# Scores in four quarters of the array, and a ring for the transposed probabilities, in a fused attention and feed-forward kernel

## The chip, the core and the metric

The kernel runs on one core of one Trainium2 chip. A core has five engines that run beside each other and wait for each other through semaphores: TensorE (PE: matrix multiplications into PSUM, with its weight loads PEld), VectorE (DVE), ScalarE (ACT), GpSimd (POOL) and SyncE (SP), which issues DMAs. The metric is the device time of one execution in microseconds (us); lower is better.

## What is computed

```python
scores = scale * np.matmul(q, k.transpose(0, 1, 3, 2))      # batch 8, heads 8, seq 576, head_dim 64
kth = np.partition(scores, -32, axis=-1)[..., -32:-31]
scores = np.where(scores >= kth, scores, -1e9)
attn = np.exp(scores - scores.max(-1, keepdims=True))
attn = attn / (attn.sum(-1, keepdims=True) + 1e-9)
x = np.matmul(attn, v)          # then (B,H,S,D) -> (B*S, H*D): 4608 x 512
h = x @ w_in                    # 512 x 2048
return (h * np.cos(h)) @ w_out  # 2048 x 512
```

Each row of scores keeps its 32 largest of 576; all else gets probability zero. All data is float32, and q, k and v reach the kernel with their axes already arranged (head_dim first for q and k).

## The kernel before

**Units and blocks.** The 4608 tokens are cut into 36 blocks of 128. A block has four units, one for each pair of heads; the 144 units go one after another. A sequence has 576 tokens, which is four and a half blocks, so 4 of the 36 blocks span two batches; their units have two entries in `parts` (64 rows of one batch, 64 of the next), all others have one.

**Scores.** `scores` (L229) computes a unit's 128 x 576 scores for two heads. The first 448 keys go to the PSUM tile `sc` (two buffers of two banks), the last 128 keys to the tile `rim` (two banks, shared). Per head one matmul contracts 64 rows of the array: for a usual unit the tile is 64*128 (64 rows of the array, all 128 columns), and the two heads use the upper and the lower rows. A unit of a two-batch block does it per batch: four matmuls of 64*64. In the traces each float32 matmul shows as two instructions. `take_scores` (L244) copies them to SBUF on ScalarE: L246 for `sc`, L250 for `rim`, where a two-batch unit has two copies of 64 rows and a usual one a single copy of 128 rows.

**Search and probabilities.** VectorE folds the row in two halves (L258, larger of each pair; GpSimd gets the smaller ones with L274 and L283) and finds the 32 largest by rounds of MAX8 (L350) and MATCH_REPLACE8 (L355). From the bounds (L363, L370: `nd`) ScalarE masks (L377, L379) and exponentiates (L387). `split` on GpSimd (L410, L412) parts the words into 16-bit halves, with the reciprocal of the sums (`rden`, L400) added as a last column block; a DMA writes them to DRAM (L438) and a transposing DMA reads them back (L444) into `pT`, which holds ten blocks of 128 columns: nine of probabilities, the tenth (index `2 * NT + 1`) the reciprocals. The first units are turned on TensorE instead (`turn`, L426 to L434). `pT` has five buffers.

**P@V.** `values` (L453) multiplies the four units of a block with v into the free part of `rim` (L469; first `v_tail`, tile 64*64, then `v`, tile 128*64). `take_values` (L475) then makes `xT` on VectorE: for each of the four units one multiply of 128 x 128 of `rim` with the tenth block of its `pT` (L481).

**Feed-forward.** `ff1` (L514) multiplies `xT` with w_in in groups of 16 matmuls into one of two PSUM banks `mm` (L530); ScalarE reads each bank twice (L544, L546); GpSimd and ScalarE make h*cos(h) (L566, L575, L585, L592); `ff2` (L595) multiplies with w_out (L605), and ScalarE takes the result out (L615).

**Order.** Each engine works through its instructions in the order in which the program issues them, one `slot` per unit. Slot i searches unit i on VectorE, makes the probabilities of unit i-1, sends off unit i-2, and spreads the feed-forward matmuls by the fixed `plan`. Scores are made in the even slots for the two units to come. In every slot with i % 4 == 2 the scores are followed by P@V of the block whose units are i-6 to i-3 (the first block's comes in slot 5), and `take_values` stands on VectorE ahead of the last search of that slot (`topk_round`, with `ahead`). ScalarE's copies for unit i+1 come after the exponentials. The framework adds the waits: instructions on different engines that touch the same PSUM bank of a tile are kept in the order of the program, even when both only read it. In SBUF it goes by the parts of a tile that are touched.

Of the kernel before, what the change touches and what calls it, by code (L numbers as in the profile page):

```python
# [10 lines left out]
F32 = mybir.dt.float32  # L11
# [4 lines left out]
ALU = mybir.AluOpType  # L16

P = 128
# [12 lines left out]
def kernel(  # L31
# [9 lines left out]
    nc = tc.nc  # L41
    ctx.enter_context(tc.manual_schedule())
    B, H, D, S = qT.shape
    DM, DF = moe_w_in.shape
    NT = S // P
    TAIL = S - NT * P
# [8 lines left out]
    consts = ctx.enter_context(tc.tile_pool(name="consts", bufs=1))  # L55
    loads = ctx.enter_context(tc.tile_pool(name="loads", bufs=6))
    work = ctx.enter_context(tc.tile_pool(name="work", bufs=2))
# [102 lines left out]

    units = []
    for t0 in range(0, B * S, P):
        parts = []
        for i, a in enumerate((t0, t0 + TAIL)):
            b, q0 = a // S, a % S
            if parts and parts[-1][0] == b:
                parts[-1][2] = P
            else:
                parts.append([b, q0, TAIL, i * TAIL])
        for hp in range(NP):  # L170
            units.append({"hp": hp, "tok": t0, "parts": parts})
    NU = len(units)
    pairs = {}
    v_tails = []
# [3 lines left out]
    def place(hp, j):  # L178

        return (hp + j) % 2  # L180
# [39 lines left out]
    SB = 448  # L220
    rim = ps.tile([P, 2, 512], F32, tag="rim", name="rim", bufs=1)
# [3 lines left out]
    def rim_bank(r0, j):  # L225

        return j if r0 == 0 else 1 - j

    def scores(u):  # L229
        sc = u["sc"] = ps.tile([P, 2, 512], F32, tag="sc", name="sc", bufs=2)  # L230
        for to, k0, k1 in ((sc, 0, SB), (sc_ends[u["n"] % 2], SB, S)):
            for b, q0, rows, r0 in u["parts"]:
                for j in range(2):
                    d = slice(j * D, (j + 1) * D)
                    st = pairs[b, u["hp"]]
                    nc.tensor.matmul(  # L236
                        to[r0 : r0 + rows, rim_bank(r0, j) if k0 else place(u["hp"], j), 0 : k1 - k0],
                        st["q"][d, q0 : q0 + rows],
                        st["k"][d, k0:k1],
                        start=True,  # L240
                        stop=True,
                    )

    def take_scores(u):  # L244
        s = u["s"] = work.tile([P, 2, S], F32, tag="s", name="s", bufs=4)
        nc.scalar.copy(out=s[:, :, 0:SB], in_=u["sc"][:, :, 0:SB])  # L246
        ends = sc_ends[u["n"] % 2]
        for r, r0 in [(slice(0, P), 0)] if len(u["parts"]) == 1 else [(slice(0, TAIL), 0), (slice(TAIL, P), TAIL)]:
            back = rim_bank(r0, place(u["hp"], 0))
            nc.scalar.copy(out=s[r, :, SB:S], in_=ends[r, :: 1 - 2 * back])  # L250

    def fold_high(u):
# [62 lines left out]
    def topk_round(u, rnd, between=(), ahead=None):  # L315
        top, rest, lasts = u["top"], u["rest"], TOPK // 8 - 1
        end = TOPK - 1 - 8 * rnd
        at = top[:, :, end : end - 8 if rnd < lasts else None : -1, 0]
        search(
            at, rest[:, :, HS:S] if rnd == 0 else rest[:, :, 0:HS], rest[:, :, 0:HS], rnd < lasts,  # L320
            between if rnd < lasts else (),
        )
        if rnd < lasts:
            return
        del u["rest"]
        low = u.pop("low")
        for k in range(TOPK // 16):
            more = k < TOPK // 16 - 1
            if ahead and not more:
                take_values(ahead)  # L330
            search(top[:, :, 1 + 8 * k : 9 + 8 * k, 1], low, low, more, () if more else between)
# [73 lines left out]
    def split(u):  # L405
# [9 lines left out]
        )  # L415
        u["halves"] = halves

    def turn(u):

        s = u.pop("s").rearrange("p j k -> p (j k)")  # L420
        pT = u["pT"] = work.tile([P, 2 * NT + 2, P], F32, tag="pT", name="pT", bufs=5)
        for half in range(2):
            tt = ps.tile([P, 512], F32, tag="mm", name="tt", bufs=2)
            for c in range(NT):
                at = (half * NT + c) * P
                nc.tensor.transpose(tt[:, c * P : (c + 1) * P], s[:, at : at + P], ident)  # L426
            nc.scalar.copy(out=pT[:, half * NT : (half + 1) * NT], in_=tt.rearrange("p (c q) -> p c q", c=NT))
        at = 2 * NT * P
        nc.tensor.transpose(room[0][:, P : 2 * P], s[:, at : at + P], ident)
        rden = u.pop("rden")  # L430
        for j in range(2):
            lhsT = rden[:, j : j + 1].to_broadcast([P, D])
            nc.tensor.matmul(room[1][j * D : (j + 1) * D, P : 2 * P], lhsT, ident, start=True, stop=True)
        nc.scalar.copy(out=pT[:, 2 * NT :], in_=rim[:, :, 3 * P :])  # L434
# [4 lines left out]

    def transposes(u):  # L440
        rows = u.pop("rows").rearrange("q h k -> (q h) k")
        pT = u["pT"] = work.tile([P, 2 * NT + 2, P], F32, tag="pT", name="pT", bufs=5)
        words = pT.rearrange("p c q -> p (c q)").bitcast(U16)
        nc.sync.dma_start_transpose(  # L444
            out=words.rearrange("p (c q) -> p c q", c=2 * NT + 2), in_=rows
        )

    def place_of(u):

        bank, at = u["hp"] % 2, u["hp"] // 2 * P  # L450
        return bank, room[bank][:, at : at + P]
# [23 lines left out]
    def take_values(us):  # L475
        blk, hp, n = block_of[us[0]["tok"]], us[0]["hp"], len(us)
        if "xT" not in blk:
            blk["xT"] = work.tile([P, NP, P], F32, tag="xT", name="xT", bufs=2)
        for i, u in enumerate(us):
            to, o, pT = blk["xT"][:, hp + i], place_of(u)[1], u.pop("pT")  # L480
            nc.vector.tensor_tensor(out=to, in0=o, in1=pT[:, 2 * NT + 1], op=ALU.mult)  # L481
        blk["left"] -= n
        blk["tick"] = ff["tick"]

# [3 lines left out]
    t0 = 0  # L488
    for w in widths:
        blk = {"t0": t0, "w": w, "left": 0, "g": [], "gated": []}  # L490
# [205 lines left out]
    for n in range(NP, len(order)):  # L696
        i = last[order[n - 6]] if n >= 6 else 0
        load_at(max(i, 2 * NP + 2), load_qk, *order[n])
        i = last_values[order[n - 2 * NP]] if n >= 2 * NP else 0
# [11 lines left out]
    def send(x):  # L711

        split(x)
        write_halves(x)
        transposes(x)
# [8 lines left out]
    def slot(i, u, w, x, z):  # L724
# [23 lines left out]
        for m in made:  # L748
            scores(m)
# [13 lines left out]
        if i + 1 < NU:  # L763
            take_scores(units[i + 1])
# [26 lines left out]
    def drain(w, x, z):  # L791

        take_banks()
        if x:
            send(x)
        if w:
            merge_first(w)
            merge_second(w)
            bounds(w)
            distances(w)  # L800
            mask(w)
            exponentials(w)
            sums(w)
            reciprocal(w)
        forward(2)
        if z:
            values(z)
            take_values(z)
        forward(2)
# [5 lines left out]
    load_qk(0, 1)  # L815
    load_weights(3, nc.sync)
    scores(units[0])
    take_scores(units[0])
    decode_first(3)
    for i in range(NU):  # L820
        ff["now"] += 1
        wq["ready"] = wq["done"]
        u, w, x = (units[i - n] if n <= i else None for n in range(3))
# [46 lines left out]
```

## Time and profile before

| | |
|---|---|
| median of 3 runs | 1422.28 us (1421.6 to 1422.38) |
| the profiled execution's own time | 1422.95 us |
| span of its profile | 1421.2 us |
| mean granted TensorE clock | 0.985 |
| busy: TensorE, VectorE, GpSimd, ScalarE | 1365.5, 1351.6, 1166.0, 1086.1 us |
| score matmuls 64*128 / 64*64 into `sc` (instructions, busy us) | 512, 133.9 / 128, 15.5 |
| the same into `rim` | 512, 53.7 / 128, 6.4 |
| L250 copies of 128 rows / of 64 rows (number, mean ns) | 128, 376 / 32, 368 |
| L481 multiplies (number, mean ns) | 144, 283 |

A row of a time line gives start, length, engine, line, operation, output<-inputs, shape and number of merged instructions; a bracket at its end says how long the engine was idle before and what ended that. Instructions of one engine overlap a little: the next one starts before the one before has ended, so the cost of an instruction in a full stream is the distance from its start to the next start, which is less than its own length. The ends of matmuls are modelled; their starts are not. A slice is a fortieth of the span, and its digit the busy share in tenths.

### The profile page before, as it was taken

The page shows a single profiled execution, that of the slowest core. Times are in us where ns is not written, and L with a number is a line of the kernel's source. Part 1 is how long each engine was busy: PE and PEld are TensorE (multiplying, and loading weights), DVE is VectorE, ACT ScalarE, POOL GpSimd, SP SyncE. Part 2 cuts the span into 40 slices and gives each one's busy share as a digit, 9 for nine tenths or more (in the row PEclk, how much of TensorE's full clock was granted, in tenths as well). Part 3 has the DMA queues.
Part 4 walks back from the last instruction along what each step waited for, and adds up shares of the span by engine and source line. Part 5 has one row for each costly group of instructions (what it writes and reads, how often), then busy time and mean ns, then how long its engine had stood idle before and what let it go on. Part 6 is the DMA issues. An engine that isn't in the chain of part 4 may idle for free.

```text
span 1421.2 us, 30370 instructions
## 1 busy us (share of the span) xinstructions
PE 1365.5 (96%) x10304; PEld 993.8 (70%) x10304; DVE 1351.6 (95%) x5233; ACT 1086.1 (76%) x1922; POOL 1166.0 (82%) x804
## 2 busy tenths in 40 slices
PE   6558999999999999999999999999999999999998
PEld 3346677777777777777777777777777777777775
DVE  7999999999999999999999999999999999999931
ACT  7877787778877788778777887777877778877741
POOL 4778888888888888888888888888888898888810
PEclk9788999999999999999999999999999999999999
DMA  9576766656665666556665566756766565565530
GB/s 287 189 214 174 200 199 171 172 165 195 167 175 146 171 183 170 169 158 198 173 181 146 149 183 179 181 155 180 190 164 167 153 173 158 153 155 145 151 101 16
DMA packets 427437, 240.02 MB, mean 169 GB/s; under 512 B 375952, under 2 KB 392592, under 8 KB 427280
## 3 DMA queue, kind: packets, MB, share of 16 engines
q1 hardware_dynamic: 420720, 224.22, 58.9%
q10 hardware_dynamic: 6560, 13.85, 2.7%
q8 instruction: 81, 1.33, 0.4%
q14 instruction: 76, 0.62, 0.1%
HBM read 45.09 MB, written 101.19 MB: 103 GB/s over the span
## 4 chain that ended last, share of the span: by engine, by line
PE 92%; DVE 6%; ACT 1%; POOL 0%; DMA 0%; issue 0%; POOLq 0%
PE o L605 36%; PE mm L530 35%; PE rim L469 11%; PE sc L236 8%; DVE top L350 3%; PE rim L236 2%; DVE rest L355 1%; DVE rest L258 0%; DVE low L355 0%; DVE w_in L144 0%; DMA pT<-rows 0%; DVE w_out L144 0%; ACT s L387 0%; PE warm L813 0%; ACT s L379 0%; POOL w_out L154 0%
## 5 line engine op out<-in xcount | busy, mean ns | idle before, releaser
L530 PEld LDWEIGHTS mm<-xT,w_in 128*128 128x128 f32 x4608 | 538.4, 192 | 77.7 <-issue 63.7
L530 PE MATMUL mm<-xT,w_in 128*128 128x128 f32 x4608 | 540.2, 276 | 9.4 <-ACT x L546 7.8
L605 PE MATMUL o<-w_out,g 128*128 128x512 f32 x1152 | 524.7, 599 | 0.0
L350 DVE MAX8 top<-rest 128x8 f32<-128x288 f32 x1152 | 478.6, 450 | 0.0
L355 DVE MATCH_REPLACE8 rest<-top,rest 128x288 f32<-128x288 f32 x864 | 376.4, 443 | 0.0
L605 PEld LDWEIGHTS o<-w_out,g 128*128 128x128 f32 x1152 | 207.7, 190 | 218.0 <-issue 214.2
L410 POOL COPY halves<-s 128x2304 uint16<-128x2304 uint16 x140 | 294.8, 2105 | 58.6 <-ACT s L387 57.7
L350 DVE MAX8 top<-low 128x8 f32<-128x288 f32 x576 | 241.5, 448 | 0.5 <-POOL low L283 0.5
L387 ACT ACTIVATE s<-s,nd 128x576 f32<-128x576 f32 x288 | 220.2, 767 | 0.8
L283 POOL TENSOR_TENSOR low<-low,rest 128x576 int32<-128x576 int32 x141 | 199.4, 1414 | 11.1
L379 ACT ACTIVATE s<-s,top 128x576 f32<-128x576 f32 x288 | 205.4, 760 | 0.0
L274 POOL TENSOR_TENSOR low<-s 128x576 int32<-128x576 int32 x141 | 198.8, 1410 | 6.3 <-ACT s L250 6.3
L377 ACT ACTIVATE nd<-nd 128x2 f32<-128x2 f32 x144 | 29.3, 203 | 226.6 <-DVE nd L370 226.6
L575 POOL TENSOR_TENSOR x<-g,x 128x1024 f32<-128x1024 f32 x68 | 161.0, 2367 | 5.7
L592 POOL TENSOR_TENSOR g<-g,x 128x1024 f32<-128x1024 f32 x68 | 160.8, 2365 | 0.0
L236 PE MATMUL sc<-k,q 64*128 64x448 f32 (+1 forms) x640 | 149.4, 583 | 9.0 <-DVE low L266 4.5
L469 PE MATMUL rim<-pT,v 128*64 128x128 f32 (+1 forms) x2560 | 138.3, 267 | 0.0
L469 PEld LDWEIGHTS rim<-pT,v 128*64 128x64 f32 x2560 | 129.2, 139 | 6.5 <-issue 6.0
L246 ACT COPY s<-sc 128x896 f32<-128x896 f32 x144 | 128.3, 891 | 3.4 <-PE sc L236 3.4
L355 DVE MATCH_REPLACE8 low<-top,low 128x288 f32<-128x288 f32 x288 | 125.3, 443 | 0.0
L566 POOL TENSOR_SCALAR x<-x 128x1024 f32<-128x1024 int32 x68 | 71.3, 1048 | 61.4 <-ACT x L546 61.4
L258 DVE TENSOR_TENSOR rest<-sc,s 128x576 f32<-128x576 f32 x144 | 107.7, 748 | 7.0 <-ACT s L250 6.8
(54 smaller groups left out, 1243.3 us busy)
## 6 DMA issues: line engine op xcount, KB each, us to landing
rows<-halves SPq DMA_DIRECT2D x140, 640.0 KB, 3.0
out_dram<-ob ACTq DMA_DIRECT2D x36, 256.0 KB, 2.3
q<-in_q_dram SPq DMA_DIRECT2D x31, 288.0 KB, 3.4
st<-in_moe_w_in_dram SPq DMA_DIRECT2D x16, 512.0 KB, 6.9
v<-in_v_dram SPq DMA_DIRECT2D x32, 256.0 KB, 3.3
k<-in_k_dram SPq DMA_DIRECT2D x31, 144.0 KB, 3.4
k<-in_k_dram SPq DMA_DIRECT2D x32, 128.0 KB, 3.5
st<-in_moe_w_out_dram SPq DMA_DIRECT2D x8, 512.0 KB, 4.4
```

The lines of the kernel that those rows point to most:

```text
L236: nc.tensor.matmul(to[r0 : r0 + rows, rim_bank(r0, j) if k0 else place(u["hp"], j), 0 : k1 - k0], st["q"][d, q0 : q0 + rows], st["k"][d, k ...
L274: nc.gpsimd.tensor_tensor(out=u["low"].bitcast(I32), in0=s[:, :, 0:HS], in1=s[:, :, HS:S], op=ALU.add)
L283: nc.gpsimd.tensor_tensor(out=low, in0=low, in1=u["rest"][:, :, HS:S].bitcast(I32), op=ALU.subtract)
L350: nc.vector.max(to[:, j], src[:, j])
L355: nc.vector.match_replace(rest[:, j], to[:, j], src[:, j], NEG)
L379: nc.scalar.activation(out=s[:, j], in_=s[:, j], func=AF.Prelu, bias=less[:, j, 1:2], scale=1.0, alpha=FAR)
L387: nc.scalar.activation(out=s[:, j], in_=s[:, j], func=AF.Exp, bias=nd[:, j : j + 1], scale=SCALE, accum_out=den[:, j, 0:1],)
L410: nc.gpsimd.tensor_copy(out=halves[:, :, 0 : 2 * S], in_=s.rearrange("p (k h) -> p h k", h=2))
L469: nc.tensor.matmul(to[d, r], lhsT, rhs, start=(bank, j) not in begun, stop=c == NT - 1 and u in us[-2:] and r0 + rows == P,)
L530: nc.tensor.matmul(mm[:, at : at + w], w_in[f // FC][:, c, (f % FC) * P : (f % FC + 1) * P], blk["xT"][:, c], start=c == 0, stop=c == NC - 1,)
L575: nc.gpsimd.tensor_tensor(out=x, in0=g, in1=x, op=ALU.subtract)
L605: nc.tensor.matmul(o, g[:, at : at + P], w_out[f], start=f == 0, stop=f == NF - 1)
```

## The change

Every unit's scores run as four matmuls of 64*64 (each head, each 64 tokens), as those of two-batch units did; the list `halves_of` gives both halves their batch. L250's copy is made in two halves of 64 rows for every unit. The five buffers of `pT` become one tile `ring` with five parts, part n % 5 for unit n. Where units of a block lie next to each other in the ring, `take_values` multiplies four (when all four do) or two with one instruction; a pair that crosses the ring's end still takes two instructions.

```diff
+            halves_of.append((b, q0, i * TAIL))
...
-            for b, q0, rows, r0 in u["parts"]:
+            for b, q0, r0 in u["halves_of"]:
                 for j in range(2):
...
-                        to[r0 : r0 + rows, rim_bank(r0, j) if k0 else place(u["hp"], j), 0 : k1 - k0],
-                        st["q"][d, q0 : q0 + rows],
+                        to[r0 : r0 + TAIL, rim_bank(r0, j) if k0 else place(u["hp"], j), 0 : k1 - k0],
+                        st["q"][d, q0 : q0 + TAIL],
                         st["k"][d, k0:k1],
...
-        for r, r0 in [(slice(0, P), 0)] if len(u["parts"]) == 1 else [(slice(0, TAIL), 0), (slice(TAIL, P), TAIL)]:
-            back = rim_bank(r0, place(u["hp"], 0))
+        for r0 in (0, TAIL):
+            r, back = slice(r0, r0 + TAIL), rim_bank(r0, place(u["hp"], 0))
             nc.scalar.copy(out=s[r, :, SB:S], in_=ends[r, :: 1 - 2 * back])
...
+    RING = 5
+    ring = consts.tile([P, RING, 2 * NT + 2, P], F32, tag="ring", name="ring")
...
-        pT = u["pT"] = work.tile([P, 2 * NT + 2, P], F32, tag="pT", name="pT", bufs=5)
+        pT = u["pT"] = ring[:, u["n"] % RING]
...
-        for i, u in enumerate(us):
-            to, o, pT = blk["xT"][:, hp + i], place_of(u)[1], u.pop("pT")
-            nc.vector.tensor_tensor(out=to, in0=o, in1=pT[:, 2 * NT + 1], op=ALU.mult)
+        i = 0
+        while i < n:
+            at, h = us[i]["n"] % RING, (hp + i) // 2
+            m = 4 if n - i == 4 and at + 4 <= RING else 2 if at + 2 <= RING else 1
+            if m > 1:
+                o = rim[:, :, 2 * (S - SB) + h * P : 2 * (S - SB) + (h + m // 2) * P]
+                nc.vector.tensor_tensor(
+                    out=blk["xT"][:, hp + i : hp + i + m].rearrange("p (h b) q -> p h b q", b=2),
+                    in0=o.rearrange("p b (h q) -> p h b q", q=P),
+                    in1=ring[:, at : at + m, 2 * NT + 1].rearrange("p (h b) q -> p h b q", b=2),
+                    op=ALU.mult,
+                )
+            else:
+                for k in range(i, i + 2):
+                    nc.vector.tensor_tensor(
+                        out=blk["xT"][:, hp + k], in0=place_of(us[k])[1],
+                        in1=ring[:, us[k]["n"] % RING, 2 * NT + 1], op=ALU.mult,
+                    )
+                m = 2
+            i += m
```

More of the change, by code (lines that the diff above doesn't have):

```diff
@@ L162 @@
     for t0 in range(0, B * S, P):
-        parts = []
+        parts, halves_of = [], []
         for i, a in enumerate((t0, t0 + TAIL)):
             b, q0 = a // S, a % S
+            halves_of.append((b, q0, i * TAIL))
             if parts and parts[-1][0] == b:
@@ L170 @@
         for hp in range(NP):
-            units.append({"hp": hp, "tok": t0, "parts": parts})
+            units.append({"hp": hp, "tok": t0, "parts": parts, "halves_of": halves_of})
     NU = len(units)
@@ L441, in transposes @@
         rows = u.pop("rows").rearrange("q h k -> (q h) k")
-        pT = u["pT"] = work.tile([P, 2 * NT + 2, P], F32, tag="pT", name="pT", bufs=5)
+        pT = u["pT"] = ring[:, u["n"] % RING]
         words = pT.rearrange("p c q -> p (c q)").bitcast(U16)
```

## The prediction

> **What bounds the kernel now.** I read the page's busy times and slices first, then the busy time of one stretch, the chain of waits in order of time, VectorE's waits, and at last the time line of a few blocks. A block is one tile of 128 tokens: four units of two heads, and 36 blocks in all.
>
> ```profile
> PE 1365.5 (96%) x10304; PEld 993.8 (70%) x10304; DVE 1351.6 (95%) x5233; ACT 1086.1 (76%) x1922; POOL 1166.0 (82%) x804
> ...
> PE   6558999999999999999999999999999999999998
> ...
> DVE  7999999999999999999999999999999999999931
> ```
>
> TensorE and VectorE are both near full; shares alone don't say which one sets the pace. VectorE is full from the second slice on and stops before the end; TensorE is full from about 115 us to the end.
>
> ```profile
> 600.00:900.00 300.00, 300.00 (x2342) 219.38 (x2339) 298.32 (x1166) 236.73 (x419) 262.74 (x179) 1.00 0.64 170
> ```
>
> In the middle (columns: stretch, length, then busy TensorE, its weight loads, VectorE, ScalarE, GpSimd, granted clock) TensorE is idle for 0.00 of 300 us and VectorE for 1.68, some 0.2 per block.
>
> ```profile
> 672.47 4.24 PE rim L469 x80
> ...
> 709.43 4.24 PE rim L469 x80
> ...
> 746.38 4.24 PE rim L469 x80
> ```
>
> In the chain, P@V of one block begins 36.95 us after that of the block before, and everything between is TensorE. So TensorE sets the period. VectorE follows it at one place:
>
> ```profile
> DVE rest L258 <- ACT s L250: 6.8, 2, 6.6
> ...
> DVE xT L481 <- ACT s L250: 4.6, 10, 0.7
> ```
>
> The multiply xT (L481) waits for ScalarE's copy L250, which waits for P@V. In most blocks that wait is too small for this list, but the time line has it: the last MATCH_REPLACE8 ahead of xT starts at 713.56; after one, the next instruction normally starts 0.36 later (708.12, then 708.48), so xT could start at 713.92 and starts at 714.12. VectorE therefore waits 0.20 per block, and its own work is 36.95 - 0.20 = 36.75 us. Only 0.20 separates the two engines: a gain on TensorE counts only as far as VectorE follows.
>
> **The scores on TensorE.** The program already does for some units what the change does for all: in the four blocks that span two batches (16 of 144 units) scores run as four 64*64 matmuls. First a usual block, then one of those (start, length, engine, line, tile):
>
> ```profile
> 707.21 1.02 PE L236 MATMUL sc<-k,q 64*128 64x448 f32 x4
> ...
> 708.28 0.92 PE L236 MATMUL sc<-k,q 64*128 64x448 f32 x4
> ...
> 709.95 3.71 PE L469 MATMUL rim<-pT,v 128*64 128x128 f32 x64
> ...
> 727.81 1.02 PE L236 MATMUL sc<-k,q 64*128 64x448 f32 x4
> ...
> 729.96 1.55 PE L605 MATMUL o<-w_out,g 128*128 128x512 f32 x3
> ```
>
> ```profile
> 485.98 0.98 PE L236 MATMUL sc<-k,q 64*64 64x448 f32 x8
> ...
> 487.54 3.71 PE L469 MATMUL rim<-pT,v 128*64 128x128 f32 x64
> ...
> 505.40 0.98 PE L236 MATMUL sc<-k,q 64*64 64x448 f32 x8
> ...
> 506.42 0.93 PE L236 MATMUL sc<-k,q 64*64 64x448 f32 x8
> ...
> 507.50 0.70 PE L605 MATMUL o<-w_out,g 128*128 128x512 f32 x1
> ```
>
> Twice the instructions take about the same time, so the quarters do run at once. A block has two pairs of units. The pair followed by o: 2.15 us (727.81 to 729.96) becomes 2.10 (505.40 to 507.50), -0.05. The pair followed by P@V: its first unit goes from 1.07 (707.21 to 708.28) to 1.02 (505.40 to 506.42), its second up to the large P@V matmuls from 1.67 (708.28 to 709.95) to 1.56 (485.98 to 487.54): -0.16. Together **-0.21 per block**: 36.95 becomes 36.74. Around each of the four two-batch blocks the forms are mixed now. Of the four pairs in its two periods one gains 0.05 and one nothing; 64*128 then 64*64 takes 1.18 + 1.56 (484.80, 485.98, 487.54) and 64*64 then 64*128 takes 1.13 + 1.77 (521.71, 522.84, 524.61) up to the large P@V matmuls, and both become 1.02 + 1.56: -0.16 and -0.32. That is -0.53 in place of -0.42: 0.1 more each, 0.4 in all.
>
> In a usual unit both column halves will read the same keys; in the rows above they read two batches' keys. This no row shows. Bounds: the -0.05 of the rows, or the halves in turn, one more 1.02 per unit. I take the rows: same tile form, order and PSUM banks.
>
> Against a hope for more stands that the unsplit unit already fills all columns: the rows give 2%. The Trainium skill, "TensorEngine Tiling (Array Packing)", Overview (Theoretical Speedup), promises up to 2x where a dimension is at most 64; by that factor an estimate would be 0.5 us off each of 144 units, 72 us.
>
> **The second copy on ScalarE.** L250 copied the last 128 keys' scores once per usual unit, now in two halves, as already in two-batch units. The halves start 0.38 apart (520.04 after 519.66): +0.38 per unit. ScalarE waits for VectorE's nd in nearly every slot, 226.6 us over 138 waits or 1.6 each, which takes the 0.38 up. It is late in two places.
> - Ahead of the fold (L258). The copy ended 0.49 (705.49, 705.98) to 0.63 before it in the tightest slots; that leaves about 0.11. In a two-batch block the second copy ended at 520.41 and the fold started at 520.52, without a wait. Cost nothing; if the cover goes, up to 0.2 a block.
> - Ahead of xT, once per block:
>
> ```profile
> 714.12 0.88 DVE L481 TENSOR_TENSOR xT<-rim,pT 128x128 f32<-128x128 f32 x4
> ...
> 529.15 0.88 DVE L481 TENSOR_TENSOR xT<-rim,pT 128x128 f32<-128x128 f32 x4 [0.59 <-ACT s L250]
> ```
>
> The o after P@V starts at 713.60 and 528.25, so xT comes 0.52 and 0.90 after P@V: with two copies 0.38 later. This is a delay of VectorE against TensorE, paid once and not in each block, as long as no TensorE instruction waits for what stands behind xT. Behind xT on VectorE are the rest of the search, the fold and nd, behind nd ScalarE's exps and the PSUM reads L544 and L546. The nearest use: L546 ended at 723.26 and the matmul into that bank starts at 724.14, 0.88 later. Next, the fold that frees a score buffer ended at 706.73 (705.98 + 0.75), and the second unit's scores start at 708.28, 1.55 later. 0.38 fits in both. Cost in the middle: nothing.
>
> The skill's "PSUM — Partial Sum Buffer", on bank collisions, says that two engines reading one bank and quadrant must be kept apart, and the tiling page (PSUM Bottleneck) that the evacuation may become the bound after packing. Both speak against this change. The trace shows the first as xT's wait behind a copy that it doesn't need; priced per block it would be 32 x 0.38 = +12, by the rows 0.4 once.
>
> **The multiply on VectorE.** Four xT of 128 elements start 0.20 apart (0.80 for four, 714.12 to 714.92). One of 512 isn't in the trace. Nearest row: L258, also PSUM with SBUF, 576 elements, 0.66 from start to next start (715.97, 716.63): (0.66 - 0.20) / 448 = 1.03 ns an element and 0.07 fixed. So 512 take 0.60 and 256 take 0.33. With a ring of five, blocks go in turn 4; 1+1+2; 2+2; 2+1+1; 4: savings 0.20, 0.07, 0.14, 0.07, 0.20, mean 0.14. Bounds: 0.20 (as one now), or 4 x 0.28 = 1.13, the single's mean length. VectorE's work is then 36.75 - 0.14 = 36.61, at worst 36.68, under TensorE's 36.74. The ring itself costs nothing: the changed program's waits name the transpose into the same fifth only, and a transpose still waits for the xT of the unit five before, which is done by 715.00 where the transpose is issued at 719.47.
>
> **Start and end.** Up to 115 us VectorE leads. At 110.61 its fold started 0.03 after the copy: the second copy adds 0.38 there, the multiply at 68.23 gives 0.20 back; at 120.25 xT waits for the copies again, +0.38. TensorE then waits 0.9 for unit 11's transposed probabilities (chain: 147.99 DMA pT<-rows, 5.88). Between 0 and 1.2; I take +0.7. At the end, the matmuls at 1352.70 already wait 0.6 for L546, so VectorE's lateness passes on, less what the last merged multiply gives back: between 0 and 0.38, +0.3. No scores run after that.
>
> **Sum.** From the P@V ending at 158 us to that ending at 1342 there are 32 periods: 32 x -0.21 = -6.7, two-batch blocks -0.4, start +0.7, end +0.3: **-6.1**. The profiled execution took 1422.95 (span 1421.2), so it would take 1416.85; it lies 0.67 above the median 1422.28 of the runs: **1416.2**.
>
> **Rivals.**
> - *VectorE becomes the bound.* For: only 0.13 lies between the floors. With the multiply saving nothing the period is 36.75, -6.3, 1417; at 1.13 a block VectorE needs 37.08, +4, 1427, but no row runs so slow per element. At 0.95, midway, 36.90: -1.8 + 1.0, 1421.5: no change.
> - *The second copy is paid in each block* (slower). Place: between P@V and xT. It decides if a TensorE instruction behind xT comes under the 0.88 cushion, so that TensorE waits for ScalarE's reads. Then VectorE's loop closes over TensorE: 36.95 + 0.38 - 0.14 = 37.19, 32 x 0.24 + 1 = +8.7, 1431. Against: in two-batch blocks xT was as late, and TensorE stayed without idle time.
> - *The halves do not share the keys' stream:* 4 x 1.02 a block, +130, 1552.
> - *No gain on TensorE:* the pairs keep 2.15: head and tail alone, 1423.3.
>
> **Chances.** Forecast 0.72, 1414.5 to 1418; VectorE bound 0.15, two thirds of it still faster; second copy each block 0.06; halves in turn 0.02; no gain 0.05. About 0.2%, 2.8 us, is what a measurement of this kernel can tell from no change: faster 0.82 (0.72 + 0.10), within 0.09 (0.05 + 0.04), slower 0.09 (0.06 + 0.02 + 0.01). The range, 1414.0 to 1420.8, takes in the forecast's own range and most of VectorE bound.
>
> **What would show it.** P@V starts 36.74 apart; a pair of scores before o 2.10; the score matmuls all 64*64; xT 0.90 after P@V; xT in rows of 0.6 and 0.33; TensorE without idle time. TensorE waiting for L546 or L258 in each block would prove me wrong, as would a VectorE without any wait ahead of xT.

## The result, and the profile after

The changed kernel takes **1415.7 us** (median of 5 runs, 1414.99 to 1417.1); the kernel before, measured beside it, 1422.28 (5 runs, 1421.6 to 1422.77). The ratio is **0.9956, 95% interval 0.9946 to 0.9967**: 6.6 us faster by the medians, against a forecast of 1416.2. The profiled execution took 1416.63, with a span of 1414.8.

The busy times, the slices of TensorE and the granted clock on the page of the changed kernel:

```profile
PE 1354.5 (96%) x11328; PEld 975.1 (69%) x11328; DVE 1346.2 (95%) x5161; ACT 1143.5 (81%) x2050; POOL 1164.6 (82%) x804
...
PE   4567999999999999999999999999999999999998
...
PEclk6688999999999999999999999999999999999999
```

There are 1024 more matmul instructions, and TensorE is busy 11 us less. ScalarE is busy 57 us more, 46 of them in the copies (288 of 368 ns, 105.9 in all, in place of 48.1 and 11.8). The middle stretch (TensorE, its weight loads, VectorE, ScalarE, GpSimd, granted clock):

```profile
600.00:900.00 300.00, 300.00 (x2553) 216.44 (x2550) 299.36 (x1160) 250.68 (x447) 264.74 (x181) 1.00 0.64 172
```

TensorE still has no idle time, and VectorE has 0.64 us in 300 where it had 1.68: 0.08 per block instead of 0.2. TensorE still sets the period, but the margin is thinner. The chain of waits has P@V every 36.70 us (before 36.95):

```profile
596.94 4.08 PE rim L473 x80
633.64 4.08 PE rim L473 x80
670.34 4.08 PE rim L473 x80
```

TensorE's time line of one block shows where the 0.256 per block comes from:

```profile
504.49 0.98 PE L237 MATMUL sc<-k,q 64*64 64x448 f32 x8
505.29 0.40 PE L237 MATMUL rim<-k,q 64*64 64x128 f32 x8
...
506.59 3.70 PE L626 MATMUL o<-w_out,g 128*128 128x512 f32 x8
...
520.80 0.98 PE L237 MATMUL sc<-k,q 64*64 64x448 f32 x8
...
521.82 0.93 PE L237 MATMUL sc<-k,q 64*64 64x448 f32 x8
...
522.79 0.62 PE L473 MATMUL rim<-ring,v_tail 64*64 64x128 f32 x16
523.34 3.71 PE L473 MATMUL rim<-ring,v 128*64 128x128 f32 x64
526.98 3.27 PE L626 MATMUL o<-w_out,g 128*128 128x512 f32 x7
```

and, of the block of the kernel before whose scores the prediction shows, three more rows:

```profile
709.36 0.67 PE L469 MATMUL rim<-pT,v_tail 64*64 64x128 f32 x16
...
713.60 3.70 PE L605 MATMUL o<-w_out,g 128*128 128x512 f32 x8
...
728.66 0.39 PE L236 MATMUL rim<-k,q 64*128 64x128 f32 x4
```

The pair before o takes 2.10 from its first start to o's (before 2.15). The pair before P@V takes 1.99 (before 2.15), and P@V itself 4.19 (before 4.24). So 0.05 comes from the one place and 0.21 from the other. The 0.05 is gained by the first unit of the pair, which follows the feed-forward's 128*128 matmuls: up to its `rim` matmuls it takes 0.80 (504.49 to 505.29) in place of 0.85 (727.81 to 728.66). In the second unit, behind scores of its own form, the same stretch takes 0.752 in place of 0.754 (medians between 300 and 1300 us). So this part too is gained where the form changes.

VectorE's multiplies in a block with one merged and two single ones:

```profile
491.18 0.49 DVE L497 TENSOR_TENSOR xT<-rim,ring 128x128 f32<-128x128 f32 x2
491.58 0.41 DVE L489 TENSOR_TENSOR xT<-rim,ring 128x256 f32<-128x256 f32 x1
491.91 0.45 DVE L351 MAX8 top<-low 128x8 f32<-128x288 f32 x1
```

0.40 for two singles and 0.33 for the merged one, start to start. One merged multiply of 512 elements takes 0.60 (70.08 to 70.68). The o after this P@V starts at 490.28, so xT stands 0.90 behind P@V.

### The profile page after: what moved, and what is told of

Its sections match the earlier page's. It is cut to its first block, busy times and chain, and to the rows that moved or that the text cites. A ratio compares the mean times of both kernels' runs of the same rounds, so it can differ in the third digit from the quotient of the medians.

```text
span 1414.8 us, 32526 instructions
## 1 busy us (share of the span) xinstructions
PE 1354.5 (96%) x11328; PEld 975.1 (69%) x11328; DVE 1346.2 (95%) x5161; ACT 1143.5 (81%) x2050; POOL 1164.6 (82%) x804
## 4 chain that ended last, share of the span: by engine, by line
PE 82%; DVE 9%; ACT 6%; DMA 1%; POOL 1%; issue 0%; SPq 0%; ACTq 0%; DVEq 0%; POOLq 0%
PE o L626 32%; PE mm L551 32%; PE rim L473 10%; PE sc L237 7%; DVE top L351 4%; DVE rest L356 2%; PE rim L237 2%; DMA st<-in_moe_w_in_dram 1%; ACT s L388 1%; ACT s L380 1%; DVE rest L259 1%; ACT st L136 1%; DVE low L356 1%; ACT w_in L133 0%; ACT w_out L133 0%
## 5 line engine op out<-in xcount | busy, mean ns | idle before, releaser
L237 PE MATMUL sc<-k,q 64*64 64x448 f32 x1152 | 144.7, 570 | 12.3 <-DMA k<-in_k_dram 7.7
L473 PE MATMUL rim<-ring,v 128*64 128x128 f32 (+1 forms) x2560 | 138.3, 267 | 0.0
L473 PEld LDWEIGHTS rim<-ring,v 128*64 128x64 f32 x2560 | 129.2, 139 | 6.5 <-issue 6.0
L251 ACT COPY s<-rim 64x256 f32<-64x256 f32 x288 | 105.9, 368 | 26.6 <-PE rim L473 24.9
```

What stands on the lines that cost most here:

```text
L237: nc.tensor.matmul(to[r0 : r0 + TAIL, rim_bank(r0, j) if k0 else place(u["hp"], j), 0 : k1 - k0], st["q"][d, q0 : q0 + TAIL], st["k"][d, k ...
L473: nc.tensor.matmul(to[d, r], lhsT, rhs, start=(bank, j) not in begun, stop=c == NT - 1 and u in us[-2:] and r0 + rows == P,)
```

## The experiments

The theory (A): quarters save TensorE time mostly by taking away changes of tile form around P@V; the second copy is a delay that fits under the cushion between ScalarE's read L567 (L546 before) and the next matmul into that bank; the merged multiply only keeps VectorE below TensorE. The rivals: (B) the second copy is paid in every block, the multiply gives it back; (C) VectorE is the bound, so the multiply is what gains. Every ratio is to the kernel before on the same chip, with its 95% interval.

**The quarters alone**: both copies, but `pT` in five buffers and four multiplies, as before.

```diff
-        pT = u["pT"] = ring[:, u["n"] % RING]
+        pT = u["pT"] = work.tile([P, 2 * NT + 2, P], F32, tag="pT", name="pT", bufs=5)
...
+            nc.vector.tensor_tensor(out=to, in0=o, in1=pT[:, 2 * NT + 1], op=ALU.mult)
```

> The quarters and the two copies as in the changed kernel, but five separate buffers and four multiplies of 128 as before. Theory A (TensorE sets the period, VectorE follows 0.2 behind): TensorE alone would need 36.70 us a block as in the changed kernel, VectorE 36.75, so VectorE takes over by a hair: period 36.75, TensorE idle for some 0.05 a block, total 1417 to 1418, i.e. most of the gain is there. Theory B (VectorE sets the period and the merged multiply earns the gain): period 36.95, about 1422. Theory C (the second copy costs 0.38 in each block and the merge hides it): period 36.8 to 37.1, 1419 to 1427.

1417.7, ratio 0.9971 (0.9961 to 0.998). Most of the gain is there without the ring. The periods are 36.70 in some stretches and 36.75 in others (blocks after two-batch ones have 36.70). So no 0.38 is paid in each block here, without a merged multiply that could give it back: B falls. In the last stretch of the middle:

```profile
900.00:1200.00 300.00, 300.00 (x2469) 216.06 (x2468) 300.00 (x1176) 252.10 (x450) 264.02 (x180) 1.00 0.62 171
```

VectorE (third engine column) is full: with four multiplies it becomes the bound at 36.75, just the 36.75 which the prediction had worked out as its own work. The 0.05 is seen on TensorE as a feed-forward group that takes 3.71 to 3.73, from its first start to that of the scores behind it, in place of 3.66.

**The ring and the merged multiply alone**: scores and copies as before.

```diff
+    def pieces(u):
...
+        return u["parts"]
...
-            for b, q0, r0 in u["halves_of"]:
+            for b, q0, rows, r0 in pieces(u):
```

> The ring and the merged multiplies alone; scores and copies as before. A: period stays 36.955, VectorE only waits longer ahead of xT (0.2 becomes 0.27 to 0.4), total within 1 us of before, 1421.5 to 1422.5. B: VectorE's 0.14 a block is the gain: period 36.82, about 1418. C: with the single copy and the merge, faster than the changed kernel, 1410 or less.

1422.54, ratio 0.9998 (0.9989 to 1.0006); the period is 36.955, as before. Saving VectorE time buys nothing while TensorE sets the pace: C falls.

**Quarters only for the pairs before P@V** (below), and in another kernel **only for the pairs before o** (`in (1, 2)`); the other units have one copy again:

```diff
+        if u["n"] % NP in (3, 0):
+            return [(b, q0, TAIL, r0) for b, q0, r0 in u["halves_of"]]
+        return u["parts"]
```

> As the changed kernel, but only the units of the pair whose scores stand ahead of P@V (unit number mod 4 is 3 or 0) run in quarters; the pair ahead of o is as before. A, with the gain at the changes of form: the pair ahead of P@V keeps its 1.99 up to the first P@V matmul and P@V its 4.19, the other pair is back at 2.15: period 36.95 - 0.21 = 36.75, 1417 to 1418. If instead each pair earned alike (half of 0.255 each), period 36.83, 1420. As the record had it, 0.16 for this pair: 36.80, 1419.

1416.38, ratio 0.9967 (0.9954 to 0.998), period 36.747: 0.208 less than before. From the chain of waits:

```profile
596.14 4.08 PE rim L479 x80
632.89 4.08 PE rim L479 x80
```

> As the changed kernel, but only the pair whose scores stand ahead of o (unit number mod 4 is 1 or 2) runs in quarters. A, gain at the changes of form: this pair 2.10 in place of 2.15, the pair ahead of P@V back at 2.15 and P@V at 4.24: period 36.955 - 0.047 = 36.908; with the one with the other pair alone (36.747) the two parts add up to the whole (0.047 + 0.208 = 0.255). Total about 1421. If each pair earned alike: 36.83, 1418.

1421.22, ratio 0.999 (0.9981 to 0.9999), period 36.908: 0.047 less.

```profile
597.61 4.24 PE rim L479 x80
634.52 4.24 PE rim L479 x80
```

The two together are 0.255, the whole of the change's 0.256.

**`v_tail` after v instead of ahead of it.** If the 0.21 is saved at changes of form, then putting the one 64*64 part of P@V behind the 128*64 part should bring the changes back, with the same matmuls.

```diff
-            for c in (NT, *range(NT)):
+            for c in (*range(NT), NT):
...
-                            stop=c == NT - 1 and u in us[-2:] and r0 + rows == P,
+                            stop=c == NT and u in us[-2:] and r0 + rows == P,
```

> The changed kernel with P@V's 64*64 matmuls (v_tail) after the 128*64 ones instead of ahead of them: the same matmuls, but the scores' 64*64 is now followed by 128*64, then 64*64, then o's 128*128, one change of form more. A: the pair of scores and P@V take 0.1 to 0.2 more than 6.18 in each block, period 36.80 to 36.90, +3 to +7. Rival (the gain is in the shorter weight loads of 64 columns and not in the changes of form): period 36.70 within 0.03.

1422.28, ratio 0.9995 (0.9986 to 1.0004): the gain is gone. The period is 36.860, 0.161 more than the changed kernel's. It is still 0.095 under that of the kernel before; in the profiled execution most of the 3 us that this gives are lost at the start, where the fourth P@V begins 2.2 later (192.95 against 190.74) after a wait of 1.20 for a transposing DMA. Its time line at the same place:

```profile
523.16 0.98 PE L237 MATMUL sc<-k,q 64*64 64x448 f32 x8
...
525.26 3.71 PE L473 MATMUL rim<-ring,v 128*64 128x128 f32 x64
528.90 0.67 PE L473 MATMUL rim<-ring,v_tail 64*64 64x128 f32 x16
529.50 3.70 PE L626 MATMUL o<-w_out,g 128*128 128x512 f32 x8
```

The pair takes 2.10 instead of 1.99 and P@V 4.24 instead of 4.19, with the very same matmuls. From the scores to o this kernel changes form three times (64*64, 128*64, 64*64, 128*128), as the kernel before did (64*128, 64*64, 128*64, 128*128); the changed kernel does it twice, because scores and `v_tail` have one form. One change less is worth 0.161 here. With it the change's 0.256 adds up: 0.047 for each of the two pairs, by the run before, and 0.161 for the change of form, 0.255. Why scores of 64*64 behind the feed-forward cost 0.05 less than those of 64*128 no run separates: it can be a cheaper change of form or the shorter weight loads.

**More copies.** How far is the second copy free? Useless repeats of a copy stretch the time from P@V to xT. The first run repeats the second half's copy for the unit ahead of xT, three copies in all. The text on record speaks of four and +0.76; the kernel as run repeated only one half, +0.38, and is to be read so.

```diff
+        if u["n"] % NP == 3:
+            nc.scalar.copy(out=s[r, :, SB:S], in_=ends[r, :: 1 - 2 * back])
```

> The changed kernel with each of the two rim copies of units with number mod 4 = 3 made twice, so that four copies of 64 rows stand between P@V and xT in each block (+0.76 us of work there that has no use). A: the delay of VectorE and ScalarE against TensorE is free only within the cushion at the read L567 ahead of the next matmul into that bank, now about 0.45 from its end to that matmul, of which some 0.2 to 0.3 can be given up; so TensorE idles for 0.45 to 0.55 a block there, period 37.15 to 37.25, about +15, 1430 to 1433. C (copies are paid in full in each block): +0.76, period 37.46, 1440. If a delay is always paid only once: period 36.70, 1416 to 1417.

1418.97, ratio 0.9977 (0.9968 to 0.9985). The periods are 36.70, 36.76 and 36.82 in blocks with one, two and three multiplies. The chain of waits shows one of each, in the order one, three, two:

```profile
634.35 4.08 PE rim L475 x80
671.05 4.08 PE rim L475 x80
707.88 4.08 PE rim L475 x80
744.64 4.08 PE rim L475 x80
```

So 0.00, 0.06 and 0.12 are paid in each block. In the traces a repeat moves xT by 0.40 rather than 0.38: it starts 5.08 after P@V's first matmul in the changed kernel, 5.48 here and 5.88 with four copies. So 0.40, 0.34 and 0.28 were still free in the changed kernel, and the difference between the blocks is the 0.06 to 0.07 that a merged pair saves.

With the same two lines inside the loop over the halves, both are repeated: four copies, +0.76.

> The changed kernel with both rim copies of units with number mod 4 = 3 made twice: four copies between P@V and xT, +0.76 us. (The kernel e4_third_copy as it ran repeats only the second half's copy: three copies, +0.38, half of what its expectation counts with.) From e4's periods of 36.70, 36.76 and 36.83 in blocks with one, two and three multiplies, the cushion is 0.38, 0.32 and 0.25; A: the second 0.38 is past the cushion and is paid in full: 37.08, 37.14 and 37.21, mean 37.14, TensorE waiting for the read ahead of mm (L567 of the changed kernel), +14 against the changed kernel, 1430. Paid once only: 36.70.

1431.69, ratio 1.0059 (1.0047 to 1.0071), slower than the kernel before. The periods are 37.10, 37.16 and 37.22: 0.40, 0.46 and 0.52 more than the changed kernel, that is the 0.80 of two repeats less 0.40, 0.34 and 0.28, the cushions of the run before. Below the cushion a delay costs nothing, and beyond it all. The chain of waits of this run shows the loop that has then closed:

```profile
603.30 4.11 PE rim L475 x80
...
608.20 0.38 ACT s L251
...
608.60 0.38 ACT s L253
...
609.00 0.69 DVE xT L491
...
612.33 0.07 DVE nd L373
...
617.51 0.59 ACT x L569
...
618.15 3.84 PE mm L553 x32
```

From P@V through the copies, xT, the search, nd, the exponentials and the PSUM read (L569 there) to the matmul: the path which the prediction named as that of the slower rival.

**A copy ahead of the fold.** The other place where ScalarE could be late: the second half's copy made twice for another unit of each block, whose copies end 0.12 ahead of the fold.

```diff
+            if u["n"] % NP == 2 and r0:
+                nc.scalar.copy(out=s[r, :, SB:S], in_=ends[r, :: 1 - 2 * back])
```

> The changed kernel, with the second half's copy of the rim scores made once more (useless work, 0.38) for every third unit of a block, whose copies end only 0.12 ahead of VectorE's fold. This is the first place at which the prediction said ScalarE might be late. Theory A (VectorE waits 0.26 in front of that fold in every block; its own work per block is 36.61, so its loop is 36.61 + 0.26 = 36.87 and passes TensorE's 36.70): P@V about 36.87 apart, TensorE idle some 0.15 per block, about 1421. Theory B (the lateness is taken up once by the 0.08 to 0.2 that VectorE still has, and the search hides the rest): 36.70, 1416.

1423.17, ratio 1.0005 (0.9996 to 1.0013): the whole gain is lost to 0.38 of ScalarE time. From VectorE's waits:

```profile
DVE rest L261 <- ACT s L253: 8.3, 34, 1.0
```

8.3 us in 34 waits, 0.24 per block, close to the 0.26 that 0.38 - 0.12 gives. The median period is 36.93; over 31 periods the mean is 0.17 longer than the changed kernel's, close to 0.24 less VectorE's margin of 0.08. Theory A holds for its mechanism: a wait on VectorE of more than its margin is paid in each block. It expected about 1421; the profiled execution, the fastest of 12, took 1421.54, and why the median lies 1.6 above it isn't known.

**The start.** Units 0 to 11 as before (one copy, 64*128 scores), the rest as changed; run twice.

```diff
+        if u["n"] >= 12:
+            return [(b, q0, TAIL, r0) for b, q0, r0 in u["halves_of"]]
+        return u["parts"]
```

> As the changed kernel, but units 0 to 11 keep the two matmuls of 128 columns and the single copy. A: the start's loss goes (P@V of the third block ends at 158.0 to 158.3 in place of 159.4), the period stays 36.70: 1.2 less than the changed kernel, about 1414.5. Rival: the start is late because TensorE was granted a lower clock in its first 60 us in that execution (0.57 to 0.74 in place of 0.67 to 1.00), not because of the copies: then no difference beyond the scatter.

1418.64, ratio 0.9963 (0.9951 to 0.9974): the 1414.5 hoped for was missed, and by the time alone this kernel can't be told from the changed one (0.9946 to 0.9967).

> The kernel with units 0 to 11 as before, once more, for a second profile of its start. Theory A (the wait of 5.5 of the fourth block's P@V for a transposing DMA belongs to the order of the start as such): a fourth P@V of 9 to 10 again, middle and end as before, about 1418.5. Theory B (it was one execution): the fourth P@V takes 4.19, and the time is about 1414.

One execution, 1420.07. Both traces show the same thing. The third P@V begins at 152.2 to 152.3 (changed kernel 155.23), as meant; the fourth then waits:

```profile
188.94 0.62 PE L479 MATMUL rim<-ring,v_tail 64*64 64x128 f32 x12
193.01 0.44 PE L479 MATMUL rim<-ring,v_tail 64*64 64x128 f32 x4 [3.45 <-DMA ring<-rows]
193.38 5.38 PE L479 MATMUL rim<-ring,v 128*64 128x128 f32 x64
```

The fourth unit's transposing DMA, issued at 184.56, landed 8.40 later (7.9 in the repeat; the median of these is under 5). The head start of 3 us was given back and more, twice. So the start isn't bound by the copies alone. TensorE was earlier, but this transpose was issued when the changed kernel issues it (184.68), where it landed in 4.84 and nothing waited for it. Why it took 8 us in both runs is open.

The rival, the clock, falls with these two profiles: the first 60 us, in stretches of 20, ran at 0.74, 0.57 and 0.60 in the first and at 1.00, 0.95 and 0.59 in the repeat, and the third P@V ended at 156.43 and 156.47.

**The changed kernel once more**, for its start:

> The changed kernel once more, for a second profile of its start. If the late start belongs to the change, the third block's P@V ends again at 159.4 (before: 157.9), whatever clock is granted in the first 60 us; if it belongs to one execution's DMAs or clock, it moves by a microsecond or more.

One execution, 1417.92. The third P@V ends at 159.16 (159.42 in the first profile), so the lateness belongs to the change. The other kernels with quarters from the first unit on end it between 158.5 and 160.3, the ring alone, with the scores as before, at 158.0 (before: 157.9). But the fifth P@V waits 1.19 for a transposing DMA, where it waited for nothing in the first profile:

```profile
229.97 0.33 PE L473 MATMUL rim<-ring,v_tail 64*64 64x64 f32 x4 [1.19 <-DMA ring<-rows]
```

The kernel before has such a wait too, 0.52 at its third P@V. That they make the difference between runs of one kernel is likely, but the runs' other executions have no profile to show it.

None of the kernels tried is faster than the changed one.

## Why the prediction was right

**TensorE sets the period.** Right: no idle time before or after, and the ring alone changed nothing.

**-0.21 per block from the quarters.** The mechanism was right, the size was not: **-0.256** was measured. The pair before o gave 0.047 (forecast 0.05). The pair before P@V gave 0.208 (forecast 0.16). The step that was mis-sized is the second unit before P@V: the prediction put it at 1.56 up to the large P@V matmuls, from a row of a two-batch block where it follows a 64*128 unit, so that a change of form was still in it; behind a 64*64 unit it takes 1.52 (521.82 to 523.34). The extra 0.1 around each two-batch block came as forecast: periods of 37.00 and 37.01 became 36.70. That usual units' halves read the same keys made no difference to the rows.

The Trainium skill, "TensorEngine Tiling (Array Packing)", Theoretical Speedup, would have had up to 2x; a pair went from 2.15 to 2.10. Its Tiling Modes section (Key Properties) says that a change of the tiling mode drains TensorE. That rule, which the prediction did not weigh, agrees with the runs, which give it a size: 0.16 for the one change of form that `v_tail` ahead of v saves.

**The second copy costs nothing in the middle.** Right. ScalarE's read L567 now ends at 500.39 (start and length in its time line), and the weight load behind it waits for it:

```profile
499.71 0.68 ACT L567 ACTIVATE x<-mm,quarter 128x512 int32<-128x512 f32 x1
```

and TensorE's weight loads at the same place:

```profile
500.45 0.19 PEld L551 LDWEIGHTS mm<-xT,w_in 128*128 128x128 f32 x1 [0.29 <-ACT x L567]
500.83 0.30 PEld L551 LDWEIGHTS mm<-xT,w_in 128*128 128x128 f32 x2 [0.20 <-issue]
```

The matmul starts at 500.83, 0.44 after the read's end, where 0.88 less 0.38 would leave 0.50. TensorE waiting for this read in each block was to prove the prediction wrong; its weight loads do wait, in 36 places (before in 8), but the matmuls come no later: 3.44 behind the o group ahead of them (497.39), before 3.43 (720.71 to 724.14). The runs with three and four copies measured how much of the cushion can still be used: 0.28 to 0.40. The slack ahead of the fold is 0.12 to 0.14, forecast 0.11, and what its loss costs (up to 0.2 a block, the prediction said) came out at 0.17 on the mean.

**The merged multiply, 0.33 and 0.60.** Right to 0.01, by the step from the nearest row. Its worth was named only in part: beside keeping VectorE under TensorE (without it 36.75 in a good part of the blocks) it shortens the path from P@V to the matmul, and so is part of the cushion.

**Start +0.7, end +0.3.** Too low, and both lie over the upper bounds of 1.2 and 0.38. At the end of the third P@V, where the forecast's 32 periods begin, the changed kernel is 1.5 behind (157.92, 159.42). It is late from the first P@V on, which waits for ScalarE's copy L438; in the kernel before it starts at 60.31, after a wait of 0.47, and in the two runs with the first twelve units as before at 60.25 and 60.27. TensorE's row:

```profile
62.46 1.13 PE L473 MATMUL rim<-ring,v_tail 64*64 64x128 f32 x16 [2.64 <-ACT ring L438]
```

The first xT waits too:

```profile
70.08 0.69 DVE L489 TENSOR_TENSOR xT<-rim,ring 128x512 f32<-128x512 f32 x1 [1.61 <-ACT s L251]
```

The prediction gave back 0.20 for the multiply there and had neither wait. ScalarE was behind in these first units, and the copies' lateness counted. The end costs +0.8: some 0.5 at the wait that the prediction named, where the weight loads at 1346.10 wait 1.12 for L567 instead of 0.61. The other 0.3 is the last output DMA: from its issue to the end of the span it takes 3.5 in place of 3.2 (1411.33 and 1417.92), in one execution of each kernel, and nothing ties it to the change.

**The sum** agrees by luck, because two errors cancel: the 32 periods, two-batch blocks included, gave -8.6 (forecast -6.7 - 0.4 = -7.1), start and end +2.3 (forecast +1.0). Together -6.3, against -6.1.

**The rivals.** VectorE as the bound was 0.08 per block away, and the quarters without the ring reached it. The second copy paid in each block was real as a mechanism, and 0.28 to 0.40 away: with four copies it was 0.4 to 0.5 per block. No run showed the halves running in turn or TensorE without a gain.

## What to carry to other kernels

A small matmul's cost depends on its neighbours: count the changes of tile form around it before counting its columns, and put stretches of the same form next to each other. Work added to an engine off the path is free up to the cushion of the loop it sits in and paid in full beyond it; find that cushion at the first instruction of the pacing engine that waits for what stands behind the addition, and measure it with useless repeats, one dose below and one above. When two engines are within 0.2 of each other per period, shorten the second one in the same change, or the gain stops at its work.

## What the runs showed of the hardware

- A wait of TensorE costs more than its length when it is long enough. After the waits of 3.45 and 3.38 in the two runs with the start as before, the large P@V matmuls took 5.38 and 6.11 instead of 3.71, in a granted clock of 0.67 and 0.50. After the wait of 1.19 the clock stayed at 1.00 (228 to 232 us). The stretches after the wait of 3.38 in the repeated run (clock in the third last column):

```profile
193.00:196.00 3.00, 3.00 (x27) 2.67 (x29) 1.25 (x6) 0.00 (x0) 1.91 (x2) 0.50 0.32 132
196.00:199.00 3.00, 3.00 (x36) 3.00 (x36) 0.00 (x0) 0.00 (x0) 1.35 (x1) 0.58 0.89 178
```

  The Trainium skill, "TensorE: Matmul & The Clock Gate", Part 1, has the clock at half after an idle window of about 3.4 us; these rows agree.
- The granted clock of the first 60 us differs between executions of like kernels: 1.00, 0.95 and 0.67 in the three stretches of 20 us before, 0.74, 0.58 and 0.57 after, 0.74, 0.59 and 0.59 with the ring alone, where the scores are as before. It did not move the third P@V: with the first twelve units as before, two executions with 0.74 and 1.00 in the first stretch ended it at 156.43 and 156.47, and the ring alone ended it within 0.2 of the kernel before.
